# Splitting five late output stores in two, so that the last store uses the eighth DMA semaphore

## The chip, the cores and the metric

The kernel runs on one core of one Trainium2 chip. The metric is device time in microseconds (us) of one execution. A trace of one execution comes with each kernel; its "span" runs from the first to the last recorded instruction and is about 1.8 us shorter than the time of that same execution. Engines: PE (TensorE), DVE (VectorE), ACT (ScalarE), POOL (GpSimd), SP (the sync engine, which here issues most stores). A "q" behind a name is that engine's sequencer or queue.

## The reference

Cross attention between a sequence and a small state, for both sides, and then a gated feed-forward layer:

```python
xread = softmax(x @ state.T / sqrt(D)) @ state       # 8 batches, 8 heads, 512 rows, D = 64
sread = softmax(state @ x.T / sqrt(D)) @ x           # 32 state rows
x = concatenate([xread, sread], axis=2)              # then heads joined: 4352 rows x 512
out = (maximum(x @ w_gate, 0) * (x @ w_val)) @ w_out # d_ff = 1536; float32 output
```

## The kernel before

A batch's 512 rows leave in four groups of 128 (`tsub`): twelve matmuls fill one PSUM bank, ACT copies it to one of four `o_sb` buffers, and SP issues a store of 256 KB. The last group of the last batch is done in three column pieces, so that the very last store is a small one (64 KB):

```python
def fin_x(b, tsub, eng="act"):
    o_sb = opool.tile([128, d_model], FP32, name="o_sb", tag="o_sb")     # opool has 4 buffers
    copy[eng](out=o_sb, in_=held["o", b, tsub])
    nc.sync.dma_start(out=out_rows(b, tsub), in_=o_sb)

def fin_s(t2):                       # state rows of four batches: four stores of 32 rows
    ...
    nc.scalar.copy(out=o_sb, in_=held["o", B, t2])
    for bq in range(4):
        eng = nc.sync if bq % 2 == 0 else nc.scalar
        eng.dma_start(out=outr[t2 * 4 + bq, S:SP], in_=o_sb[bq * Ns:(bq + 1) * Ns])

def out_last(b, tsub):
    for lo, n, eng, q in ((0, 256, nc.scalar.copy, nc.scalar), (256, 128, nc.scalar.copy, nc.scalar),
                          (384, 128, nc.vector.tensor_copy, nc.sync)):
        ...                          # 12 matmuls, a copy, then the store:
        q.dma_start(out=out_rows(b, tsub)[:, cols], in_=o_sb[:, 0:n])
```

The layer under the kernel hands out semaphores. The DMAs issued from SP and ACT take eight of them in rotation, called HW0 to HW7 here, in the order of the program. At the end of the program, SP waits for all of them in an order that is fixed in the built program: two software-DMA semaphores, then HW0, HW1, and so on to HW7. Then come a drain and a barrier of all engines. There are as many issues before the end as make the last store fall on HW2.

The softmax here doesn't subtract the row's maximum and nothing guards it: scores larger than these inputs give would overflow.

Of the kernel before, what the change touches and what calls it, by code (L numbers as in the profile page):

```python
# [16 lines left out]
def kernel(  # L17
# [9 lines left out]
    nc = tc.nc  # L27

    B, H, S, D = x.shape
# [326 lines left out]
    def out_rows(b, tsub):  # L356
        return out[b * SP: b * SP + S].rearrange("(p q) m -> q p m", q=NC)[tsub]

    def fin_x(b, tsub, eng="act"):
        o_sb = opool.tile([128, d_model], FP32, name="o_sb", tag="o_sb")  # L360
        copy[eng](out=o_sb, in_=held["o", b, tsub])  # L361
        nc.sync.dma_start(out=out_rows(b, tsub), in_=o_sb)

    def fin_s(t2):
        outr = out.rearrange("(b s) m -> b s m", s=SP)
# [23 lines left out]
    def out_piece(b, i):  # L389
        out_part(b, i)  # L390
        if i % 3 == 2:
            fin_x(b, i // 3)
# [15 lines left out]
    def w_load(w, lo, n):  # L408
# [4 lines left out]
                        in_=x[0, HK:H].rearrange("h (p c) d -> p h c d", c=NC))  # L413
# [16 lines left out]
    def spin(n, cols=512):  # L430
        for i in range(n):
# [6 lines left out]
             "sc": att_sc, "ex": att_exp, "nr": att_sum, "nx": att_scale, "aT2": att_T2, "ao2": att_out2, "aT": att_T, "ao": att_out,  # L438
             "c": c_unit, "co": c_out, "u": u_unit, "uo": u_out, "gv": gv, "re": relu, "mu": mult, "o": out_part,
             "of": fin_x, "xn": x_next, "xp": x_pad, "sr": sr_mm, "sn": sr_norm}  # L440
    program = """
    dx.1.0.2 dx.1.1.2 stc.0.0.act stc.0.1.dve xc.0.0.act dw.0.0.128 spin.6 stT.0@5 xT.0.0@0 xc.0.1.dve dw.1.0.128 on
# [86 lines left out]
    for g in range(first, NF * (B + 1)):  # L529
        b, jf = divmod(g, NF)  # L530
# [47 lines left out]
```

## Time and profile before

| what | value |
|---|---|
| time, median of the first three runs | 224.28 us (224.14 to 224.79) |
| span of the profiled run | 222.95 us |
| PE busy | 98% of the span |
| last matmul ends, by PE's closing drain | 219.75 us |
| last store issued / landed | 220.11 / 221.74 us |
| SP's first drain at the end | 222.12 us |

PE carries the kernel until 219.75, and no store is on that path. The 3.2 us behind it are a fixed sequence: copy, issue, landing, waits, barrier. The lines that show it are in the prediction. A store is recorded twice: its issue on SP's queue (0.33 us for 128 rows) and, much later, the increments of its semaphore when the data has landed. The stores of before, from the list of DMA issues (count, KB each, median us from issue to landing):

```profile
out_dram<-o_sb SPq DMA_DIRECT2D x31, 256.0 KB, 2.4
out_dram<-o_sb SPq DMA_DIRECT2D x5, 64.0 KB, 1.7
out_dram<-o_sb ACTq DMA_DIRECT2D x5, 64.0 KB, 2.0
```

### The profile page before, as it was taken

The page shows a single profiled execution, that of the slowest core. Times are in us where ns is not written, and L with a number is a line of the kernel's source. Part 1 is how long each engine was busy: PE and PEld are TensorE (multiplying, and loading weights), DVE is VectorE, ACT ScalarE, POOL GpSimd, SP SyncE. Part 2 cuts the span into 40 slices and gives each one's busy share as a digit, 9 for nine tenths or more (in the row PEclk, how much of TensorE's full clock was granted, in tenths as well). Part 3 has the DMA queues.
Part 4 walks back from the last instruction along what each step waited for, and adds up shares of the span by engine and source line. Part 5 has one row for each costly group of instructions (what it writes and reads, how often), then busy time and mean ns, then how long its engine had stood idle before and what let it go on. Part 6 is the DMA issues. An engine that isn't in the chain of part 4 may idle for free.

```text
span 222.9 us, 4842 instructions
## 1 busy us (share of the span) xinstructions
PE 217.4 (98%) x1959; PEld 106.9 (48%) x1959; DVE 131.1 (59%) x233; ACT 123.2 (55%) x233; POOL 48.9 (22%) x54
## 2 busy tenths in 40 slices
PE   6999999999999999999999999999999999999994
PEld 2554454444544444444444444444444445666543
DVE  2399998965695559664877368646875433222100
ACT  4498788843567555574466456645654444222221
POOL 8877654300603334015000700000000000000000
PEclk9999999999999999999999999999999999999999
DMA  6999999152046771771169114511311111111132
GB/s 154 183 195 197 208 232 284 39 121 97 0 124 209 119 260 62 164 247 50 50 134 281 56 50 97 97 47 47 94 50 47 47 49 50 49 69 72 51 94 94
DMA packets 37799, 25.48 MB, mean 114 GB/s; under 512 B 18864, under 2 KB 33200, under 8 KB 37776
## 3 DMA queue, kind: packets, MB, share of 16 engines
q1 hardware_dynamic: 24912, 16.85, 26.3%
q0 software_dynamic: 11968, 7.47, 21.5%
q10 hardware_dynamic: 896, 0.85, 1.5%
q8 instruction: 15, 0.25, 0.4%
q14 instruction: 8, 0.07, 0.1%
HBM read 18.35 MB, written 8.91 MB: 122 GB/s over the span
## 4 chain that ended last, share of the span: by engine, by line
PE 95%; ACT 2%; DMA 1%; issue 0%; DVE 0%; DVEq 0%; ACTq 0%
PE o_ps L353 39%; PE gv_ps L316 38%; PE gv_ps L333 5%; PE up L291 4%; PE sc_ps L200 2%; DMA st_f<-in_state_dram 1%; PE sr_ps L264 1%; PE upc L291 1%; PE o_ps L379 1%; PE warm_ps L432 1%; PE xT_ps L186 1%; PE stT_ps L129 1%; PE xT_ps L169 1%; PE xT_ps L173 0%; ACT xT L189 0%; ACT e_sn L207 0%
## 5 line engine op out<-in xcount | busy, mean ns | idle before, releaser
L316 PE MATMUL gv_ps<-ans,U 128*128 128x512 bf16 x384 | 94.6, 379 | 0.3 <-ACT ans L249 0.3
L353 PE MATMUL o_ps<-wo_sb,h_sb 128*128 128x512 bf16 x372 | 94.8, 379 | 0.0
L340 ACT ACTIVATE g_sb<-gv_ps 128x512 bf16<-128x512 f32 (+1 forms) x108 | 62.5, 581 | 50.1 <-PE gv_ps L316 39.1
L344 DVE TENSOR_TENSOR h_sb<-gv_ps,g_sb 128x512 bf16<-128x512 f32 x96 | 64.7, 688 | 41.5 <-ACT g_sb L340 40.7
L316 PEld LDWEIGHTS <-U 128*128 128x128 bf16 x384 | 36.1, 98 | 40.7 <-issue 0.9
L353 PEld LDWEIGHTS <-h_sb 128*128 128x128 bf16 x372 | 35.3, 98 | 40.0 <-issue 1.6
L361 ACT COPY o_sb<-o_ps 128x512 f32<-128x512 f32 x29 | 17.1, 590 | 16.2 <-PE o_ps L353 16.2
L301 ACT CAST U<-up 128x512 bf16<-128x512 f32 x37 | 19.2, 594 | 11.1 <-PE up L291 11.1
L301 DVE CAST U<-up 128x512 bf16<-128x512 f32 x35 | 22.0, 682 | 2.3 <-PE up L291 1.9
L142 POOL CAST xb<-xf 128x1024 bf16<-128x1024 f32 x10 | 10.1, 1042 | 55.7 <-DMA xf<-in_x_dram 48.4
L256 POOL COPY xa<-xb 128x2048 bf16<-128x2048 bf16 (+1 forms) x9 | 15.6, 1748 | 13.9 <-issue 13.7
L213 DVE TENSOR_REDUCE cs<-e_sn 128x16 f32<-128x512 bf16 x16 | 10.9, 678 | 8.9 <-ACT e_sn L207 8.9
L344 DVE TENSOR_TENSOR hs_sb<-gv_ps,g_sb 128x256 bf16<-128x256 f32 x12 | 5.1, 425 | 15.3 <-PE gv_ps L333 10.5
L207 ACT ACTIVATE e_sn<-sc_ps 128x512 bf16<-128x512 f32 x16 | 9.7, 604 | 4.7 <-PE sc_ps L200 4.6
L219 DVE TENSOR_TENSOR a_sn<-e_sn,rc 128x512 bf16<-128x512 bf16 x16 | 11.4, 723 | 0.3
L291 PEld LDWEIGHTS <-stT 64*32 64x32 bf16 x512 | 5.9, 90 | 9.5 <-issue 8.1
L311 ACT CAST U<-upc 128x512 bf16<-128x512 f32 (+1 forms) x18 | 8.7, 542 | 0.9 <-PE upc L291 0.9
L200 PEld LDWEIGHTS <-xT 128*128 128x128 bf16 x128 | 5.9, 102 | 3.7 <-ACT xT L189 0.4
L291 PE MATMUL up<-wg_sb,stT 64*32 64x512 bf16 x144 | 7.5, 381 | 0.0
L432 PE MATMUL warm_ps<-hs_sb 128*128 128x512 bf16 x15 | 6.2, 548 | 1.2 <-DVE hs_sb L396 1.2
L333 PE MATMUL gv_ps<-br,wg_sb 128*128 128x256 bf16 x48 | 7.2, 273 | 0.0
L333 PE MATMUL gv_ps<-br,wv_sb 128*128 128x256 bf16 x48 | 7.2, 273 | 0.0
(65 smaller groups left out, 126.9 us busy)
## 6 DMA issues: line engine op xcount, KB each, us to landing
out_dram<-o_sb SPq DMA_DIRECT2D x31, 256.0 KB, 2.4
xf<-in_x_dram SPq DMA_DIRECT2D x4, 1024.0 KB, 6.1
wo_sb<-in_moe_w_out_dram POOLq DMA_DIRECT2D x2, 768.0 KB, 14.7
wg_sb<-in_moe_w_gate_dram POOLq DMA_DIRECT2D x5, 256.0 KB, 8.7
wv_sb<-in_moe_w_val_dram POOLq DMA_DIRECT2D x5, 256.0 KB, 9.3
xf<-in_x_dram POOLq DMA_DIRECT2D x1, 1024.0 KB, 15.4
xb<-in_x_dram POOLq DMA_DIRECT2D x3, 256.0 KB, 6.0
xb<-in_x_dram POOLq DMA_DIRECT2D x1, 512.0 KB, 11.7
```

Source lines behind the costliest of these rows:

```text
L200: nc.tensor.matmul(ps[:, :, c, jj], xT[b][:, c, 2 * jp + jj], stT[:, b, 2 * jp + jj], start=True, stop=True)
L213: nc.vector.reduce_sum(out=cs, in_=e_v, axis=AX.X)
L219: {"dve": nc.vector, "pool": nc.gpsimd}[eng].tensor_tensor(out=by_pair(a_sn[b], jp).rearrange("p r (j n) -> p r j n", n=Ns), in0=e_v, in1= ...
L256: nc.gpsimd.tensor_copy(out=v[:, hs:hs + src.shape[1]], in_=src)
L291: nc.tensor.matmul(dst[parity][32 * j:32 * j + 32], stT[r:r + 64, b, j, 32 * parity:32 * parity + 32], wsb[r:r + 64, j, lo:lo + n], start= ...
L301: copy[eng](out=U[b][:, w, kc, lo:lo + 512], in_=held["u", b, w, lo][kc])
L316: nc.tensor.matmul(ps[w], U[b][:, w, kc, f0:f0 + 128], ANS[b][:, kc].rearrange("p c t -> p (c t)"), start=(kc == 0), stop=(kc == NK - 1))
L333: nc.tensor.matmul(ps[w][:, 0:nt], wsb[:, j, f0:f0 + 128], br[:, j].rearrange("p b n -> p (b n)"), start=(j == 0), stop=(j == NJ - 1))
L340: nc.scalar.activation(out=g_sb[:, 0:n], in_=ps[0][:, 0:n], func=AF.Relu)
L344: nc.vector.tensor_tensor(out=dst, in0=ps[1][:, 0:n], in1=held["g", b, jf][:, 0:n], op=ALU.mult)
L353: nc.tensor.matmul(held["o", b, tsub], src[:, jf, tsub * 128:(tsub + 1) * 128], wo_sb[:, jf], start=(jf == 0), stop=(jf == NF - 1))
L361: copy[eng](out=o_sb, in_=held["o", b, tsub])
```

## The change

Five stores become ten, five more issues turn the rotation by five, and the last store moves from HW2 to HW7, the last semaphore that SP asks for.

```diff
     def fin_x(b, tsub, eng="act"):
         o_sb = opool.tile([128, d_model], FP32, name="o_sb", tag="o_sb")
         copy[eng](out=o_sb, in_=held["o", b, tsub])
-        nc.sync.dma_start(out=out_rows(b, tsub), in_=o_sb)
+        n = 2 if b == B - 2 or (b == B - 1 and tsub == 0) else 1
+        for i in range(n):
+            rows = slice(128 // n * i, 128 // n * (i + 1))
+            nc.sync.dma_start(out=out_rows(b, tsub)[rows], in_=o_sb[rows])
```

## The prediction

> **What bounds the kernel now.** I read the page's busy shares first, then the chain of waits, then only the last five microseconds, because the diff touches only output stores near the end.
>
> The page's busy line and the chain's summary by engine:
>
> ```profile
> PE 217.4 (98%) x1959; PEld 106.9 (48%) x1959; DVE 131.1 (59%) x233; ACT 123.2 (55%) x233; POOL 48.9 (22%) x54
> ...
> PE 95%; ACT 2%; DMA 1%; issue 0%; DVE 0%; DVEq 0%; ACTq 0%
> ```
>
> TensorE is busy for 98% of the 222.9 us span and 95% of the chain is its matmuls. The change touches no matmul, so nearly all of the time is out of its reach. What is left is the tail. The chain of waits, cut to the end of the span (start us, length us, what):
>
> ```profile
> 208.42 8.63 PE o_ps L353 x40
> 217.05 2.66 PE o_ps L379 x36
> 219.72 0.03 DVEq L382
> 219.75 0.04 issue
> 219.79 0.29 DVE o_sb L382
> ```
>
> The last matmul ends at 219.7, VectorE copies the last 128x128 piece until 220.08, and the listed chain stops there. The span ends at 222.95, though: 2.9 us follow in which no engine computes. They belong to the sync engine's queue. Its waits from 216 us on (waiter, releaser, total us, times, longest us):
>
> ```profile
> SPq L383 <- DVE o_sb L382: 2.0, 1, 2.0
> SPq L362 <- ACT o_sb L361: 1.7, 1, 1.7
> SPq L573 <- DMA out_dram<-o_sb: 1.0, 2, 0.6
> SPq L573 <- PEq L573: 0.7, 2, 0.5
> ```
>
> L573 is the end of the program: there SP waits twice for output stores to land, 1.0 us together. Asked for line 573 on SP in three windows (220.4 to 221.7, 221.7 to 222.1, 222.1 to 223), the trace answers (durations ns min/median/max, first and last start us):
>
> ```profile
> L573 SPq EVENT_SEMAPHORE  x3: 28/28/28, 220.5 to 221.3; - x3
> ```
>
> ```profile
> L573 SPq EVENT_SEMAPHORE  x6: 28/28/28, 221.8 to 222.1; - x6
> ```
>
> ```profile
> L573 SPq DRAIN  x3: 7/7/7, 222.1 to 222.4; - x3
> ```
>
> So nine wait instructions stand in a row: three spread over 0.8 us, then six packed into 0.3 us. The built program says what they are. HW0 to HW7 below are the eight semaphores that stores from SP and ACT use in rotation. At the end SP waits first for two software-DMA semaphores, then in eight instructions for HW0, HW1, ... HW7 in that fixed order (each paired with one other, long satisfied). The trace's record of each instruction: HW0 passes at 220.693, HW1 at 221.294, HW2 at 221.754, HW3 at 221.816, HW4 at 221.875, HW5 at 221.937, HW6 at 221.996, HW7 at 222.058; the drain follows at 222.123 and the closing barrier after it. The records of landings say why. The last three stores sit on HW0, HW1 and HW2 and land at 220.676, 221.278 and 221.738; each wait passes 16 or 17 ns after its landing. HW3 to HW7 had landed by 219.724, so these five waits hold nothing back and still cost their time, after the last store has landed and with nothing beside them. **That is the only piece the change can take.**
>
> **What the Trainium skill says.** "Perfetto Trace Analysis", section Per-engine timelines (sequencer-only instruction): the reported start is when the semaphores are satisfied and the reported length is the execution alone. The trace agrees: a wait is reported as 28 ns, but the starts of satisfied ones are 59 to 62 ns apart, so the spacing is the cost and not the 28 ns. "Advanced Engine Details and Errata", section Miscellaneous Facts (Network/Comms): reading a semaphore from the sequencer takes 50 to 100 ns on trn2; the measured 60 ns lies in it. "DMA: Bandwidth & Descriptors", section Anatomy of one DMA: a transfer has a fixed cost of about 2.0 us (fitted on the software path), mostly the write receipt, which the semaphore has to wait for. Here the last store takes 220.113 to 221.738, 1.63 us, for 64 KB; that time stays. The same page, section Rules for kernel authors: two transfers of disjoint partition halves serialize, so splitting buys no bandwidth. No store of before is split in this way, so the trace does not show that; I don't count on a faster store.
>
> **The change part by part.** Five stores (all four of batch 6 and the first of batch 7) become two of 64 rows each. This adds five issues on SP and removes none; TensorE's, VectorE's and ScalarE's work stays. The program grows by five copies on SP and one wait instruction each on ACT and DVE, since a buffer now has two stores to wait for.
>
> *Gain.* Five more issues turn the rotation by five: the last three stores move from HW0, HW1, HW2 to HW5, HW6, HW7. The built program of the changed kernel confirms it: the very last store is on HW7, and the end block's order is unchanged. After the last landing, five waits disappear: HW2 at 221.754 to HW7 at 222.058 is 0.304 us, 5 x 60.8 ns. They move into time in which SP waits anyway: SP starts its end block at 220.510, and nine waits at 61 ns would have reached HW7 at 220.510 + 8 x 0.061 = 221.0, against a landing at 221.738. The 0.74 us of slack swallow them. Gain on the path: **0.304 us**.
>
> *Cost of the issues.* A 128-row store occupies SP for 0.332 us. My estimate is that a half costs about 0.35 more (the 32-row stores took 0.315 to 0.414). In this stretch the stores are issued at 183.9, 189.1, 194.3, 199.5 and 204.7, one per 5.2 us, and nothing but later stores stands behind them on SP. Off the path: 0.
>
> *Cost of later landings.* The whole stores land in 1.8 to 2.4 us here (204.720 to 206.726 for the last). If the second half comes 0.4 us later, that is about 2.4 us. ACT's copies reuse a buffer four copies later; for the last split one that is the copy at 217.09, ten microseconds on. ScalarE also idles before these copies waiting for TensorE (six waits, 6.4 us in total). Off the path: 0. The extra wait on ACT lies in such an idle 2.0 us; the one on DVE can run between 217.5 and 219.7, while DVE waits for the last matmul. 0 each.
>
> *Sum.* 224.28 - 0.30 = **223.98 us**, 0.14% less. The span should go from 222.95 to about 222.64.
>
> **Rivals.** (1) *The barrier waits for someone else*, so the five waits were hidden: gain 0, 224.28. Against it: PE's closing drain ends at 219.749, VectorE's at 220.137, ScalarE's at 220.174, GpSimd's barrier step comes at 222.213, 32 ns after SP's drain at 222.181. SP is the last to arrive. (2) *The halves disturb something*: ScalarE's buffer wait, or five more transfers among the store traffic. For it: twice as many issues. Against it: ten microseconds of slack on the buffers and a DMA share of 39% or less in the windows after 210. Should one 60 ns wait slip in front of the last copy, the gain would be 0.24 (224.04); a TensorE bubble of one issue, 0.35 us, would turn it into 224.3. (3) *The landing of the last store varies by more than the gain.* The three stores of the last line took 1.6, 1.6 and 1.9 us. That makes single runs unequal, not a lasting shift; it decides whether 0.3 us can be seen at all. (4) *The turned rotation makes a late store wait for a recent one*: the last twelve issues still take the semaphore of the issue eight before, which is the same pair for all that follow the first four small stores; those four now follow halves landed long before. 0.
>
> **Range and chances.** Three runs of before spread over 224.14 to 224.79, so a median may be off by 0.2 to 0.3 either way, as much as the effect. Around 223.98 I give 223.55 to 224.45. A move of 2% would be 4.5 us, fifteen times the mechanism, and no cost found comes near it: within 2% 0.98, 0.01 on either side.
>
> **What would show it.** In the changed profile, whose line numbers are three higher (L573 is L576): the waits at the end after the last landing drop from six to one; the SP drain starts about 0.08 us after that wait and not 0.37; SP waits for landings twice there still, a shorter sum of about 0.8 us (0.4 for HW6, now reached later, and 0.4 for HW7); stores of L362 become ten of 64 rows and 26 of 128; the chain to 220.08 keeps its numbers within 0.1. It would be wrong if the last landing comes later by 0.3 us or more after its issue (rival 3), if SP is still in earlier waits at the last landing, or if ScalarE's copies show waits for stores.

## The result, and the profile after

The changed kernel takes 223.75 us (median of 6 runs, 223.56 to 224.35), before took 224.12 us (6 runs, 223.92 to 224.79). The ratio is 0.9986 with a 95% interval of 0.9968 to 1.0004. Ratios here are the mean time of one kernel's fast runs over that of the other's fast runs of the same rounds, so not quite the ratio of the medians. The tail of the trace shows more.

The list of DMA issues of the changed kernel: 26 whole stores and ten halves.

```profile
out_dram<-o_sb SPq DMA_DIRECT2D x26, 256.0 KB, 2.4
out_dram<-o_sb SPq DMA_DIRECT2D x10, 128.0 KB, 2.4
```

SP's waits from 216 us on, in the changed kernel (waiter, releaser, total us, times, longest us; L576 is the end of the program, L573 before):

```profile
SPq L386 <- DVE o_sb L385: 2.0, 1, 2.0
SPq L365 <- ACT o_sb L361: 1.7, 1, 1.7
SPq L576 <- DMA out_dram<-o_sb: 0.8, 2, 0.4
SPq L576 <- PEq L576: 0.7, 2, 0.5
```

Only the third line differs from before: 0.8 us of waiting for stores to land instead of 1.0. SP comes to HW6 later and so waits less for it. The instructions of the end block on SP, in three windows (219.7 to 220.8, 220.8 to 221.06, 220.8 to 223; durations ns min/median/max, first and last start us):

```profile
L576 SPq EVENT_SEMAPHORE  x8: 28/28/28, 219.8 to 220.6; - x8
```

```profile
L576 SPq EVENT_SEMAPHORE  x1: 28/28/28, 221.0 to 221.0; - x1
```

```profile
L576 SPq DRAIN  x3: 7/7/7, 221.1 to 221.4; - x3
```

Eight of the nine waits now stand before the last landing and one after it; before, three stood before it and six after it. The records of the single instructions: the last store lands at 221.021, HW7 passes at 221.038, the drain follows at 221.103. From the last landing to the drain it is 0.082 us, against 0.385 us (221.738 to 222.123) before. **The difference is 0.303 us; 0.304 was predicted.**

The span, however, is 221.94 us and thus 1.01 us shorter, not 0.31. The remaining 0.7 us show in the chain of waits of the changed kernel, cut to its end:

```profile
216.33 2.67 PE o_ps L382 x36
218.99 0.04 DVEq L385
219.03 0.04 issue
219.07 0.29 DVE o_sb L385
```

Everything stands 0.72 us earlier than before (VectorE's last copy at 219.07 instead of 219.79), with the same lengths. Going backwards through ACT's instructions in both traces, this distance stays at 0.72 us all the way from the late copies to 35.5 us, and it arises only before that, where neither program has reached a split store. The first sign of a distance is the first work on the loaded state, on ACT, in the timeline of before and then of the changed kernel (start us, length us, instruction, idle time before it and what ended it):

```profile
3.98 0.51 ACT L121 ACTIVATE st_b<-st_f,odd 128x256 bf16<-128x256 f32 x1 [0.82 <-DMA st_f<-in_state_dram]
```

```profile
3.42 0.51 ACT L121 ACTIVATE st_b<-st_f,odd 128x256 bf16<-128x256 f32 x1 [0.25 <-DMA st_f<-in_state_dram]
```

The load arrived 0.56 us sooner. That alone does not make the 0.72 us: the distance grows to 1.5 us at about 10 us and shrinks again in steps, at 17 and at 35 us. Whether it is chance is the first question for the experiments.

Two lines of the profile could mislead. The busy share of PE is now lower:

```profile
PE 213.5 (96%) x1930; PEld 106.1 (48%) x1959; DVE 131.0 (59%) x233; ACT 123.3 (56%) x233; POOL 48.9 (22%) x54
```

The program has 1959 matmuls; 29 records are missing, as the counts beside the weight loads (1959) show; the second trace of the unchanged kernel (e1 below) has 1930 records too. And ACT's waits from 185 us on now name a store, which the prediction had listed as a sign that it was wrong:

```profile
ACT o_sb L370 <- PE o_ps L353: 2.0, 1, 2.0
ACT o_sb L370 <- DMA out_dram<-o_sb: 2.0, 1, 2.0
```

In before, both waits of this line are for PE:

```profile
ACT o_sb L367 <- PE o_ps L353: 4.0, 2, 2.0
```

The second copy's separate wait for the stores passed at 212.69 in the changed kernel though, and the copy started at 213.78, 2.590 us after the copy before it. In before the same two copies start 2.590 us apart too (211.908 and 214.498). A wait for several semaphores is put down to one of them, here the wrong one; nothing was held up.

### The profile page after: what moved, and what is told of

Read it like the earlier page. It is cut to its first block, busy times and chain, and to the rows that moved or that the text cites. A ratio compares the mean times of both kernels' runs of the same rounds, so it can differ in the third digit from the quotient of the medians.

```text
span 221.9 us, 4820 instructions
## 1 busy us (share of the span) xinstructions
PE 213.5 (96%) x1930; PEld 106.1 (48%) x1959; DVE 131.0 (59%) x233; ACT 123.3 (56%) x233; POOL 48.9 (22%) x54
## 4 chain that ended last, share of the span: by engine, by line
PE 83%; DMA 12%; POOL 2%; issue 2%; DVE 0%; POOLq 0%; DVEq 0%
PE o_ps L353 38%; PE gv_ps L316 31%; DMA st_f<-in_state_dram 5%; PE gv_ps L333 5%; PE up L291 4%; DMA wv_sb<-in_moe_w_val_dram 4%; DMA xb<-in_x_dram 3%; PE sc_ps L200 1%; PE o_ps L382 1%; PE sr_ps L264 1%; POOL st_b L124 1%; POOL xb L415 0%; PE stT_ps L129 0%; POOL xb L423 0%; PE aT_ps L235 0%
## 5 line engine op out<-in xcount | busy, mean ns | idle before, releaser
L316 PE MATMUL gv_ps<-ans,U 128*128 128x512 bf16 x372 | 93.6, 379 | 1.0 <-ACT ans L249 0.3
L353 PE MATMUL o_ps<-wo_sb,h_sb 128*128 128x512 bf16 x358 | 92.0, 379 | 1.7 <-issue 1.6
L291 PE MATMUL up<-wv_sb,stT 64*32 64x512 bf16 x144 | 7.1, 380 | 0.0
```

The source lines that it names most:

```text
L291: nc.tensor.matmul(dst[parity][32 * j:32 * j + 32], stT[r:r + 64, b, j, 32 * parity:32 * parity + 32], wsb[r:r + 64, j, lo:lo + n], start= ...
L316: nc.tensor.matmul(ps[w], U[b][:, w, kc, f0:f0 + 128], ANS[b][:, kc].rearrange("p c t -> p (c t)"), start=(kc == 0), stop=(kc == NK - 1))
L353: nc.tensor.matmul(held["o", b, tsub], src[:, jf, tsub * 128:(tsub + 1) * 128], wo_sb[:, jf], start=(jf == 0), stop=(jf == NF - 1))
```

## The experiments

**Theory.** A satisfied wait behind the last landing costs about 61 ns, and the change takes five of them off the path; splitting as such costs and gains nothing; everything else between two profiles is the start of the run. **Rivals.** (a) The splitting moved the middle of the kernel, and the 0.7 us are its doing. (b) Smaller late stores help by themselves. (c) The splits cost something that hides part of the gain.

The last column but one is read from the records of single instructions: from the last landing to SP's first drain. The last one runs from the start of ACT's last ReLU of the state rows (208.02 us in before) to the end of the span; it leaves the start of the run out.

| kernel | last store on | satisfied waits after it | ratio to before (95%) | landing to drain, us | last ReLU to end, us |
|---|---|---|---|---|---|
| before | HW2 | 5 | | 0.385 | 14.93 |
| changed | HW7 | 0 | 0.9986 (0.9968 to 1.0004) | 0.082 | 14.64 |
| e1_before_again | HW2 | 5 | 0.9995 (0.9975 to 1.0015) | 0.385 | 14.93 |
| e2_after_again | HW7 | 0 | 0.9985 (0.9962 to 1.0008) | 0.082 | 14.64 |
| e3_split8 | HW2 | 5 | 0.9996 (0.9976 to 1.0016) | 0.385 | 14.95 |
| e4_merge3 | HW7 | 0 | 0.9973 (0.9956 to 0.999) | 0.081 | 14.69 |
| e5_split6 | HW0 | 7 | 0.9999 (0.9978 to 1.002) | 0.516 | 15.07 |
| e6_split4 | HW6 | 1 | one run | 0.143 | 14.71 |
| e7_early5 | HW7 | 0 | 0.9981 (0.9959 to 1.0002) | 0.082 | 14.62 |
| e8_pack5 | HW7 | 0 | 0.9977 (0.9954 to 0.9999) | 0.082 | 14.64 |

### e1: the kernel before, against itself

No edit.

> Control: the kernel before, unchanged, against itself. Ratio 1.000 within 0.001 to 0.002; this says how much two equal kernels differ. In its trace the last store sits on HW2: from the last landing to the first drain 0.385 us (0.016 + 5 waits of 61 ns + 0.065), whatever the start does. Theory of the start: the moment at which ScalarE's copies of the middle stand moves by several tenths of a us from one profile to the next although the program is the same; the rival (the split moved the middle by the 0.72 us seen) expects it to stand where the first profile of before had it, within 0.1 us.

The ratio is 0.9995, and the tail is 0.385 us again. Its timeline at the start of ACT:

```profile
3.43 0.51 ACT L121 ACTIVATE st_b<-st_f,odd 128x256 bf16<-128x256 f32 x1 [0.27 <-DMA st_f<-in_state_dram]
```

The unchanged program did here what the changed one had done: from 35.5 us on it ran 0.85 us ahead of its own first profile. So rival (a) falls; the 0.72 us belong to the start of that run and not to the change. Why the loads of the first 35 us arrive at different times was not looked into.

### e2: the changed kernel again, on the same chip

No edit.

> The changed kernel again, on the same chip as the control. Theory: landing to drain 0.082 us, time 0.30 us less than before (ratio 0.9986). Rival (the split moves work in the middle too): 0.7 to 1.0 us less (ratio 0.9955 to 0.997).

The ratio is 0.9985 and the tail 0.082 us. Its profiled run had a slow start: its span of 223.08 us is longer than both profiles of before (222.95 and 222.10), and yet from the last ReLU to the end it takes 14.64 us, as the first profile of the changed kernel did. One trace's span would have shown the change as a loss.

This trace also shows that the first load does not decide the start. ACT's first work on the state begins as early as in the changed kernel's first trace:

```profile
3.42 0.51 ACT L121 ACTIVATE st_b<-st_f,odd 128x256 bf16<-128x256 f32 x1 [0.24 <-DMA st_f<-in_state_dram]
```

But at 17 us PE waits 0.79 us for a weight load, 0.36 us in the changed kernel's first trace, and from 35.5 us on this run is 0.43 us behind the first profile of before:

```profile
17.06 0.30 PE L291 MATMUL upc<-wv_sb,stT 64*32 64x256 bf16 x8 [0.79 <-DMA wv_sb<-in_moe_w_val_dram]
```

### e3: all of the splitting, none of the rotation

```diff
-        n = 2 if b == B - 2 or (b == B - 1 and tsub == 0) else 1
+        n = 2 if b == B - 2 or (b == B - 1 and tsub == 0) or (b == B - 3 and tsub > 0) else 1
```

> Eight late stores split, so that the last store is back on HW2, the third semaphore in the end block's order: all of the splitting and none of the rotation. Theory: landing to drain 0.385 us as in before, ratio 1.000 (within the control's noise). Rival 1 (split stores are themselves what helps): ratio 0.9986 or less. Rival 2 (splits cost a little and hide part of the gain): ratio over 1.000, for instance 1.001 if each of eight extra issues cost 0.03 us on the path.

The ratio is 0.9996. The waits at the end, from 221.19 to 221.55 us, are again six after the last landing at 221.195:

```profile
L576 SPq EVENT_SEMAPHORE  x6: 28/28/28, 221.2 to 221.5; - x6
```

Eight split stores with the last store on HW2 are neither better nor worse than whole ones, so rivals (b) and (c) have no support: from the last ReLU to the end it takes 14.95 us against 14.93, and in time less than 0.2% would not show.

### e4: all of the rotation, none of the splitting, by merging

Put into `fin_s` of before, three issues fewer, which also leads to HW7:

```diff
+        if t2 == 0:
+            nc.sync.dma_start(out=outr[0:4, S:SP], in_=o_sb)
+            return
         for bq in range(4):
```

> Nothing split: instead the four 32-row stores of the first state tile become one store, three issues fewer, which turns the rotation backwards by three and puts the last store on HW7 too. All of the rotation and none of the splitting. Theory: landing to drain 0.082 us, ratio 0.9986, as the changed kernel. Rival (the gain comes from smaller or more stores): ratio 1.000 or more. The merged store may land some us later than its parts did (its outermost dimension is 4), but nothing needs it before 219 us.

The tail is 0.081 us and the time 0.9973. The tail is as expected. What was not expected is that this store disturbs its neighbours. The issue to landing times of the other small stores (line 373 here, and line 370 of before):

```profile
DMA to landing us min/median/max: 3.7/3.8/4.0
```

```profile
DMA to landing us min/median/max: 1.6/1.9/2.0
```

The merged store itself landed 6.1 us after its issue (211.61 to 217.74), and its semaphore shows four increments at landing (217.07 to 217.74) and one at 212.69, before any data had landed, where others show sixteen. The Trainium skill, "DMA: Bandwidth & Descriptors", section Why a DMA increments its semaphore by 16 and not by 1, says that the slowest dimensions of both sides decide how many engines carry a transfer, and that the sequencer writes the missing increments at once; an outermost dimension of four gives four engines. The trace agrees with the count. VectorE reuses the buffer of the second state tile for its last copy and so waits for these late stores: its copy starts 0.112 us after PE's closing drain, instead of 0.044 to 0.048 in every other trace here. That is a loss of about 0.07 us on the path, and from the last ReLU to the end it takes 14.69 us and not 14.64. That its ratio is the lowest of all is therefore not a sign of a better kernel; the intervals overlap with the changed kernel's.

### e5: overshooting by one

```diff
-        n = 2 if b == B - 2 or (b == B - 1 and tsub == 0) else 1
+        n = 2 if b == B - 2 or (b, tsub) in ((B - 1, 0), (B - 3, 3)) else 1
```

> Six late stores split: the last store overshoots to HW0, the first of the eight in the end block, so seven satisfied waits follow its landing instead of five. Theory (61 ns for each wait behind the last landing): landing to drain 0.082 + 7 x 0.061 = 0.51 us, 0.12 us more than before, ratio 1.0005. Rival (more splits help): ratio 0.998 or less.

The last store falls on HW0. From 221.3 to 221.82 us, all eight waits stand after the landing at 221.341:

```profile
L576 SPq EVENT_SEMAPHORE  x8: 28/28/28, 221.4 to 221.8; - x8
```

The tail is 0.516 us (0.51 expected): (0.516 - 0.082) / 7 = 62 ns for each satisfied wait. In time the expected 0.12 us cannot be seen (ratio 0.9999, interval 0.9978 to 1.002).

### e6: stopping one short

```diff
-        n = 2 if b == B - 2 or (b == B - 1 and tsub == 0) else 1
+        n = 2 if b == B - 2 else 1
```

> Four stores split: the last store on HW6, one satisfied wait behind it. Only the trace's tail is read. Theory: landing to drain 0.082 + 0.061 = 0.143 us. Rival (the end is one step, either hidden or not): 0.082 or 0.385.

One satisfied wait stands behind the last store's own, from 221.15 to 221.26 us:

```profile
L576 SPq EVENT_SEMAPHORE  x2: 28/28/28, 221.2 to 221.2; - x2
```

The tail is 0.143 us, as expected: 61 ns for one wait. With 0, 1, 5 and 7 waits the tail is 0.082, 0.143, 0.385 and 0.516 us, a straight line.

### e7: five splits in the middle of the kernel

```diff
-        n = 2 if b == B - 2 or (b == B - 1 and tsub == 0) else 1
+        n = 2 if b == 3 or (b == 4 and tsub == 0) else 1
```

> Five stores split in the middle of the kernel (all of batch 3 and the first of batch 4), where transposes and loads of x stand behind them on SP; the late stores are whole again. Theory (only the place in the rotation matters): landing to drain 0.082 us, ratio 0.9986. Rival (it must be the late stores that are split): 1.000. A third outcome: the pairs of issues, 1.1 us on SP instead of 0.33, delay a load or a transpose that TensorE needs, ratio over 1.000; then ScalarE's copies in the middle come later against those around 36 us.

The tail is 0.082 us and the ratio 0.9981, though the late stores are whole. The third outcome did not come: on ACT the distance to the first profile of before is constant from 35.5 us to the end. Only the count of issues matters, and not which stores supply it.

### e8: packing instead of splitting

The four stores of batch 5 become one of 1 MB, put into `fin_x` of before. A first version with a pool of its own did not build: 8 KB per partition were needed and 0.66 KB were left. So it takes the buffer of an input that is dead by then:

```diff
+        if b == B - 3:
+            if tsub == 0:
+                held["w"] = xin.tile([128, NC, d_model], FP32, name="o_wide", tag="xf")
+            copy[eng](out=held["w"][:, tsub], in_=held["o", b, tsub])
+            if tsub == NC - 1:
+                nc.sync.dma_start(out=out[b * SP: b * SP + S].rearrange("(p q) m -> p q m", q=NC), in_=held["w"])
+            return
```

> The four stores of batch 5 packed into one of 1 MB with 128 partitions outermost (8 KB in a row), in the place of a dead input buffer: three issues fewer, the last store on HW7, nothing split and the small stores untouched. Theory: landing to drain 0.082 us, ratio 0.9986; the small stores land in 1.7 to 2.0 us again and VectorE's last copy starts 0.044 us after the end of TensorE's closing drain, as in before, and not 0.11 us after it as with the merged small store. Rival (small-store merging had other gains, its ratio being 0.9973): this one stays at 0.9986 while the merged one keeps 0.9973.

The tail is 0.082 us, the ratio 0.9977, the small stores (line 377) are undisturbed, and VectorE's last copy starts 0.044 us after PE's closing drain:

```profile
DMA to landing us min/median/max: 1.6/1.9/2.0
```

It gives the same tail with three issues fewer instead of five more. No version was clearly better than the changed kernel: whether the merged small store stays apart at 0.9973, as the rival expected, can't be decided with intervals of 0.002 either way.

All timed kernels whose last store is on HW7 have ratios of 0.9973 to 0.9986, and the three on HW2 or HW0 0.9995 to 0.9999. The four on HW7 without the disturbance of e4 average 0.9982 (the mean of 0.9986, 0.9985, 0.9981 and 0.9977), the two controls on HW2 (0.9995 and 0.9996) 0.99955: the distance of 0.0013 times 224.3 us is 0.30 us, the size of the tail's 0.303 us. With intervals of 0.002 such close agreement is partly luck, the more so as the ratios are not independent: e1 to e4 ran on one chip and share one set of 11 runs of before, e5 to e8 on another with theirs. The tail is the proof, and the times do not contradict it.

## Why the prediction was right

- **What bounds the kernel.** Right: PE sets the end of the compute, and only the tail behind it changed. PE's closing drain to VectorE's copy takes 44 to 48 ns in all traces but e4's.
- **The gain.** Right in mechanism and size: 0.304 us predicted, 0.303 measured in both traces of the changed kernel. Taking one satisfied wait as 61 ns was right for 1, 5 and 7 of them.
- **The waits fit into SP's idle time.** Right: HW5 passed at 220.171 and SP then waited for HW6 (220.550) and HW7 (221.038). The landing waits sum to 0.8 us, as stated.
- **Cost of the issues.** The term was mis-sized, though nothing came of it. A half was put at 0.35 us of SP's time. In the changed kernel's trace, the first half took 0.47 to 0.55 and the second 0.57 to 0.60, so a pair takes about 1.05 us where a whole store took 0.33. SP had 5.2 us for each, so the total stays 0; e3 shows it for eight pairs.
- **Cost of later landings.** The whole stores of this stretch were read as 1.8 to 2.4 us; the trace of before has 2.0 to 2.4. The last of them was put at 2.0 and a second half at about 2.4 us. Most second halves took 2.3 to 3.0 us, but that of the last split store 3.9 us in the changed kernel and 3.4 to 4.0 in e2, e3 and e5. Why is open. In the changed kernel it landed at 208.46 us, and its semaphore and its buffer were next asked for at 214.8 and 216.4 us, so nothing waited.
- **Rivals.** (1) The barrier: refuted as argued; from SP's first drain to the end every trace has 0.825 to 0.848 us. (2) Disturbance: absent. (3) was right that single runs differ by more than the gain, but named the wrong place. The last store's issue to landing is 1.62 or 1.63 us in all ten traces; the 1.9 us in the prediction's comparison was the larger 128 KB store. What varies is the start: ACT's last ReLU stands anywhere between 207.1 and 208.4 us. (4) The turned rotation made no store wait.
- **What would show it.** Right on the six waits that become one, the 26 and ten stores and the 0.8 us. Wrong on two: the chain "keeps its numbers within 0.1" (it moved by 0.72 us with the start, so the span was 221.94 and not 222.64), and ACT's line naming a store, which turned out to be an attribution and not a wait. The "0.08 us" from the last wait to the drain was also loosely put: 0.082 us is from the landing; from the wait it is 0.065 us.

The median came out at 223.75 us, 0.23 us below the 223.98 predicted. Of this, 0.16 us is that before itself measured 224.12 in six runs and not 224.28.

## What to carry to other kernels

After the last transfer has landed, every instruction left in the closing sequence is on the path, even a wait that is long satisfied: 61 to 62 ns for each one here. If semaphores are asked for in a fixed order, let the transfer that lands last be the one asked for last; the count of issues before it can be adjusted anywhere in the program, also by issuing fewer. For effects of a tenth of a per cent, compare a stretch between two marks in the trace and not the spans: here the start of a run moved the span by over 1 us, and a gain of 0.3 us was exact to some nanoseconds in the tail.

## What the Trainium skill lacked or had wrong

- "Advanced Engine Details and Errata", section Miscellaneous Facts, gives 50 to 100 ns for reading a semaphore, which fits; no page says that satisfied wait instructions in a row cost SP 59 to 69 ns each, start to start, although the profile reports each as 28 ns. Behind the last landing the runs show 61 to 62 ns on average.
- "DMA: Bandwidth & Descriptors", section Anatomy of one DMA, gives the fixed cost of about 2.0 us for the software path and no such figure for a store that SP issues. For the 64 KB store that SP issues last, the runs show 1.62 to 1.63 us from issue to landing, in all ten traces.
- The same page, section Rules for kernel authors, advises against splitting by partition halves because they serialize. No page has that the issues get longer: 0.47 to 0.60 us for 64 rows against 0.33 us for 128 rows.
- The same page, section Why a DMA increments its semaphore by 16 and not by 1, explains how many engines a transfer uses, and the count of four for the merged store agrees. No page has a figure for what this does to others: the small stores behind it landed after 3.7 to 4.0 us instead of 1.6 to 2.0 us. All sixteen increments of each came late, at 216.8 us or later, and not only those of four engines; why is open.
